# Quarter-array matmuls with transposed outputs in the 512-token steps of a convolution-and-gated-MLP kernel

## The chip, the cores and the metric

The kernel runs on one core of a Trainium2 chip. The metric is the device time of one execution in microseconds; the number given for a kernel is the median of its runs. TensorE is PE in the profile, its weight loads are PEld, VectorE is DVE, ScalarE is ACT, GpSimd is POOL, and SP is the queue that issues most of the transfers.

## The reference, cut to what matters

```python
# x [8, 4096, 192], weight [8 heads, 7 taps], w_in [192, 2048], w_out [2048, 192], beta [2048]
w   = softmax(weight, axis=-1)                 # one set of taps for each head of 24 channels
a   = causal_conv(x, w)                        # out[t] = sum_k w[head, k] * x[t - 6 + k]
h   = a.reshape(32768, 192) @ w_in             # [32768, 2048]
g   = h * sigmoid(beta * h)
out = g @ w_out                                # [32768, 192]
```

## The kernel before, in words

The 32768 tokens are cut into two streams of 16384 (`NS = 2`, index `s`). At every moment the kernel works on the same stretch of both streams. The 192 channels are split as channel = 3 q + k, with k from 0 to 2 (`NK`) and q from 0 to 63. So the activations of one stream fill 64 partitions in three slices, stream 0 in partitions 0 to 63, and stream 1 in 64 to 127. The weights `w_in_s` and `w_out_s` are kept in bf16 in SBUF; `w_out_s` is divided by beta, since the activation is taken as silu(beta h).

There are 37 steps: 0 and 1 of 128 tokens, 2 to 8 of 256, and 9 to 36 of 512 tokens of each stream. The F dimension of 2048 is worked in 16 chunks of 128 (`NF`, index `fc`). In a step of the main loop, for each chunk:

- `mm1(i, fc)` (L321) makes h for the chunk. The contraction of 192 is three matmuls of 64 rows a stream. The two streams use the two row halves of the array, so a pair of matmuls, 64 rows by 128 columns each, runs side by side and writes two PSUM banks (`ph`, two buffers of two banks).
- ScalarE (L324) turns the two banks at once (128x1024) into `g` in bf16.
- `mm2(i - 1, ...)` (L358) works on the step before. Its stationary operand is a block of `g` (128 tokens), its moving operand `w_out_s` (192 columns). Each contraction of 128 rows is cut into two row halves of 64, which again run side by side: while the upper half adds to one token block, the lower half adds to another (`po`, two buffers of two banks). The two halves then change places, in a second phase. `mm2_plan` spreads these pairs over the 16 chunks of the step: eight pairs a chunk where the step before has 512 tokens, four where it has 256.

`store` (L366, L372) copies a finished pair of token blocks from PSUM to `o_sb` with VectorE, and SP sends it out, tokens on partitions, in rows of 768 bytes. The last step has no step after it; `last` (L381, L384, L385) runs its second product alone, with all 128 rows at once.

VectorE makes the convolution for coming steps: `conv_ops` begins a step with a copy of the halo (L280), then for each tap a scale (L289) or a multiply-add (L291) over `acc`, and the last tap writes `xc`. In 512-token steps each tap is three instructions of 128x512, one for each slice k. `cast_x` (L84) casts loaded x to bf16 (`xb`), `transpose_x` (L95) lets SP transpose it into `xt`, and `load_x` (L78) loads x two tiles of 512 ahead.

The order on every engine is the order of the program (`pin`). VectorE's work is a list (`work`), and `vector_work` hands it out by a budget in nanoseconds: each chunk adds 1307 x tokens / 512, each item takes off its estimated cost, and items may belong to at most two steps ahead. At the end of a step everything that the next step needs is flushed out. Copies out of PSUM stand in VectorE's queue where the program finishes a pair of blocks.

Of the kernel before, what the change touches and what calls it, by code (L numbers as in the profile page):

```python
# [10 lines left out]
FP32 = mybir.dt.float32  # L11
# [8 lines left out]
def kernel(  # L20
# [19 lines left out]
    NS = 2  # L40
    TS = B * S // NS
    TILE = 512
    NB = TILE // 128

    def pin(ins):

        return tc.keep_in_program_order(ins)
# [7 lines left out]
    xt_pool = ctx.enter_context(tc.tile_pool(name="xt", bufs=3))  # L55
    acc_pool = ctx.enter_context(tc.tile_pool(name="acc", bufs=2))
    xc_pool = ctx.enter_context(tc.tile_pool(name="xc", bufs=3))
    g_pool = ctx.enter_context(tc.tile_pool(name="g", bufs=2))
    osb_pool = ctx.enter_context(tc.tile_pool(name="osb", bufs=4))
    psum_h = ctx.enter_context(tc.tile_pool(name="psum_h", bufs=2, space=bass.MemoryType.PSUM))  # L60
    psum_o = ctx.enter_context(tc.tile_pool(name="psum_o", bufs=2, space=bass.MemoryType.PSUM))

    steps = [(0, 128), (128, 128), (256, 256)]
    NP = len(steps)
    steps += [(t, 256) for t in range(TILE, 4 * TILE, 256)]
    steps += [(t, TILE) for t in range(4 * TILE, TS, TILE)]
    n_steps = len(steps)

# [30 lines left out]
    w_in_v = moe_w_in.rearrange("(q k) f -> q k f", k=NK)  # L101
    w_out_f = consts.tile([128, NF, D], FP32, name="w_out_f")
    w_out_s = consts.tile([128, NF, D], BF16, name="w_out_s")
    w_out_v = moe_w_out.rearrange("(c p) d -> p c d", p=128)

    def half_of(s):
        return slice(64 * s, 64 * s + 64)
# [47 lines left out]
    for b in (0, 2):  # L155
        for s in range(NS):
# [5 lines left out]
    ident2 = consts.tile([128, NS, Q], FP32, name="ident2")  # L162
    pin(nc.vector.tensor_tensor(out=ident2, in0=ident[:, None, 0:Q].to_broadcast([128, NS, Q]),
                                in1=ident[:, None, Q:].to_broadcast([128, NS, Q]), op=ALU.add))
    def po_tile():
        return psum_o.tile([128, 2, TILE], FP32, name="po")

    idle = psum_h.tile([128, 2, TILE], FP32, name="ph")

# [57 lines left out]
        else:  # L227
            pin(eng.tensor_scalar_mul(dst, src, rsum))  # L228

    def banks(po):  # L230
        return [po[:, 0, :], po[:, 1, :]]

    new_xt(0)
    pa = po_tile()
    t = transpose_0(pa[:, 0, :], 0)
    take_0(t, 0, act=True)
    warm(4, 128)
    for k in range(2, K):
# [5 lines left out]
        for s in range(NS):  # L244
            copy_w_in(s, HF * s + f, HF * s + f + 512)
    pin(nc.scalar.activation(scrap, one, AF.Silu))
    pb = po_tile()
    b0 = [cv0[:, 0, :], pb[:, 0, :]]
    conv_0(b0, 0)
    evac_0(b0, 0, 0, nc.scalar)  # L250
    evac_0(b0, 0, 1, nc.vector)
# [1 line left out]
    pin(nc.tensor.transpose(beta_ps, beta16, ident[0:NF, 0:NF]))  # L253
    beta = consts.tile([128, NF], FP32, name="beta")
    pin(nc.vector.tensor_copy(beta, beta_ps))
    t = transpose_0(pa[:, 0, :], 1)
    take_0(t, 1)
    halo_0(t, 1)
    rbeta = consts.tile([128, NF], FP32, name="rbeta")
# [3 lines left out]

    def scale_w_out(c):
        pin(nc.vector.tensor_scalar_mul(w_out_s[:, c, :], w_out_f[:, c, :], rbeta[:, c:c + 1]))


    def conv_ops(i):
# [45 lines left out]
                                     scale=beta[:, fcs[h]:fcs[h] + 1]))  # L314

    def mm1(i, fc):
        n = steps[i][1]
        ph = psum_h.tile([128, NS, TILE], FP32, name="ph")
        for kk in range(NK):
            for s in range(NS):  # L320
                pin(nc.tensor.matmul(ph[:, s, 0:n], w_in_s[half_of(s), kk, ts(fc, 128)],  # L321
                                     xc_of[i][half_of(s), kk, 0:n],
                                     start=(kk == 0), stop=(kk == NK - 1)))
        pin(nc.scalar.activation(g_of[i][:, fc, :, 0:n], ph[:, :, 0:n], AF.Silu,  # L324
                                 scale=beta[:, fc:fc + 1]))

    def pairs_of(i):
        nb = steps[i][1] // 128
        if nb == 1:
            return [((0, 0), (1, 0))]  # L330
        return [((s, b), (s, b + 1)) for s in range(NS) for b in range(0, nb, 2)]

    def mm2_plan(i):


        prs = pairs_of(i)
        if len(prs) == 1:
            order = [(prs[0], 0, 2 - 2 * i, 6), (prs[0], 1, 10, 16)]
        elif len(prs) == 2:
            order = [(prs[p], ph, 8 * ph + 4 * p, 8 * ph + 4 * p + 4) for ph in range(2) for p in range(2)]  # L340
        else:
            order = [(prs[2 * h + p], ph, 8 * h + 4 * ph + 2 * p, 8 * h + 4 * ph + 2 * p + 2)
                     for h in range(2) for ph in range(2) for p in range(2)]
        plan = [[] for _ in range(NF)]
        for pr, ph, u0, u1 in order:
            for n in range(NF):
                plan[u0 + n * (u1 - u0) // NF].append((pr, ph, n))
        return plan

    def mm2(i, pr, phase, fc):  # L350
        if phase == 0 and fc == 0:
            po_of[pr] = psum_o.tile([128, 2, TILE], FP32, name="po")
        po = po_of[pr]
        for half in range(2):
            q = half ^ phase
            s, b = pr[q]
            r = half_of(half)
            pin(nc.tensor.matmul(po[:, q, 0:D], g_of[i][r, fc, s, ts(b, 128)], w_out_s[r, fc, :],  # L358
                                 start=(phase == 0 and fc == 0), stop=(phase == 1 and fc == NF - 1)))
        if phase == 1 and fc == NF - 1:  # L360
            store(i, pr, po)

    def store(i, pr, po):
        t0 = steps[i][0]
        o_sb = osb_pool.tile([128, 2, D], FP32, name="o_sb")
        pin(nc.vector.tensor_copy(o_sb, po[:, :, 0:D]))  # L366
        (sa, ba), (sb, bb) = pr
        if sa == sb:
            dst = os_[sa, t0 + 128 * ba:t0 + 128 * (bb + 1), :].rearrange("(b p) d -> p b d", p=128)
        else:  # L370
            dst = os_[:, t0 + 128 * ba:t0 + 128 * (ba + 1), :].rearrange("s p d -> p s d")
        pin(nc.sync.dma_start(out=dst, in_=o_sb))  # L372

    def last(i):

        t0, n = steps[i]
        for s in range(NS):
            for b in range(n // 128):
                po = psum_o.tile([128, 2, TILE], FP32, name="po")
                for fc in range(NF):  # L380
                    pin(nc.tensor.matmul(po[:, 0, 0:D], g_of[i][:, fc, s, ts(b, 128)], w_out_s[:, fc, :],  # L381
                                         start=(fc == 0), stop=(fc == NF - 1)))
                o_sb = osb_pool.tile([128, 2, D], FP32, name="o_sb")
                pin(nc.vector.tensor_copy(o_sb[:, 0, :], po[:, 0, 0:D]))  # L384
                pin(nc.sync.dma_start(out=os_[s, t0 + 128 * b:t0 + 128 * (b + 1), :], in_=o_sb[:, 0, :]))  # L385


# [11 lines left out]
    for i in range(NP, n_steps):  # L399
        j = steps[i][0] // TILE + 1  # L400
        if i == NP + 1 or (i > NP + 1 and steps[i][0] % TILE == 0):
            if j * TILE < TS:
                work += fetch(i, j)
        work += conv_ops(i)
    budget = 0.0

    def vector_work(i, ns, flush=False):


# [4 lines left out]
            work.pop(0)[2]()  # L414
        budget = min(budget, 0.0) if work else 0.0

    EVAC = 560
    for i in range(n_steps):
        plan = mm2_plan(i - 1) if i else [[] for _ in range(NF)]
        g_of[i] = g_pool.tile([128, NF, NS, TILE], BF16, name="g")  # L420
        if i == 0:
            cv1, cv2, cv3 = banks(pb), banks(pa), banks(pb)
            for u in range(NF // 2):
                mm1_pair(0, u)
                if u == 0:
                    t = transpose_0(pb[:, 0, :], 2)
                    take_0(t, 2)
                    halo_0(t, 2)
                elif u == 1:
                    t = transpose_0(pa[:, 0, :], 3)  # L430
                    take_0(t, 3)
                    halo_0(t, 3)
                    conv_0(cv1, 1, 0, 1)
                elif u == 2:
                    conv_0(cv1, 1, 1, 4)
                elif u == 3:
                    conv_0(cv1, 1, 4, K)
                    for s in range(NS):
                        evac_0(cv1, 1, s, nc.vector)
                elif u == 4:  # L440
                    conv_0(cv2, 2, 0, 2)
                elif u == 5:
                    conv_0(cv2, 2, 2, 5)
                    for c in range(4):
                        scale_w_out(c)
                elif u == 6:
                    conv_0(cv2, 2, 5, K)
                    for s in range(NS):
                        evac_0(cv2, 2, s, nc.vector)
                elif u == 7:  # L450
                    for c in range(4, 8):
                        scale_w_out(c)
            continue
        if i < NP:
            for u in range(NF // 2):
# [8 lines left out]
                    for s in range(NS):  # L464
                        evac_0(cv3, 3, s, nc.vector)
                elif i == 1 and u == 6:
                    pt = po_tile()
                    new_xt(1)
                    for b in range(2):
                        t = transpose_0(pt[:, b, :], b, xf_of[1])  # L470
                        pin(nc.vector.tensor_copy(  # L471
                            xt_of[1][:, :, LEAD + 128 * b:LEAD + 128 * b + 128], t))
                elif i == 1 and u == 7:
# [13 lines left out]
        for u in range(NF):  # L487
            mm1(i, u)
            for t in plan[u]:
                mm2(i - 1, *t)  # L490
                if t[1] == 1 and t[2] == NF - 1:
                    budget -= EVAC
            vector_work(i, 1307 * steps[i][1] // TILE, flush=u == NF - 1)
    assert not work
    last(n_steps - 1)
# [28 lines left out]
```

## Time and profile before

| | |
|---|---|
| median of 9 runs | 695.87 us (695.45 to 697.47) |
| profiled execution | 696.23 us, of which the profile's span is 694.4 us |
| granted TensorE clock | 1.00 throughout |
| busy: PE, PEld | 687.1 us (99%), 537.7 us (77%) |
| busy: ACT, DVE | 587.5 us (85%), 542.4 us (78%) |
| DMA, mean over the span | 97 GB/s |

The busy time of a group is the union of its instructions, and the mean ns is the length of one from its start to its end. For TensorE these lengths overlap, since matmuls are pipelined and two run side by side; what counts there is the distance from one start to the next. A figure behind the last bar of a group is the engine's idle time just before its instructions, with what ended most of it. The chain that ended last runs back from the final store; an engine's share of it is the time for which it was what everything else depended on.

### The profile page before, as it was taken

To read this page: it belongs to the slowest core of one execution; us is meant where nothing else is said; L and a number is where in the kernel's file an instruction comes from. 1 tells how busy PE (TensorE), PEld (TensorE's weight loads), DVE (VectorE), ACT (ScalarE), POOL (GpSimd) and SP (SyncE) were. 2 spreads that over 40 slices of the span, in tenths; PEclk is the share of its full clock that TensorE was granted. 3 is DMA by queue.
4 is the path that set the end of the run, shared out by engine and by line. 5 is a ranking of instruction groups with operands and counts; after the bars stand their busy time and mean duration, and the time that the engine had idled before them with its cause. 6 is when DMAs were issued, how large, how long until landed. Compare 5 with 4: busy or idle time off the path is not lost.

```text
span 694.4 us, 25426 instructions
## 1 busy us (share of the span) xinstructions
PE 687.1 (99%) x11561; PEld 537.7 (77%) x11561; DVE 542.4 (78%) x905; ACT 587.5 (85%) x600; POOL 14.5 (2%) x26
## 2 busy tenths in 40 slices
PE   8999999999999999999999999999999999999998
PEld 6699986777777777777777777777777777777777
DVE  4799899999988788778788778797788797785002
ACT  6799999888888888888888888888888888888882
POOL 8000000000000000000000000000000000000000
PEclk9999999999999999999999999999999999999999
DMA  9564333444323334323334233334323432211112
GB/s 221 130 144 116 109 110 94 115 129 123 110 66 104 95 103 115 83 76 104 98 105 115 73 90 100 98 104 116 80 77 104 99 105 70 60 36 47 36 37 69
DMA packets 120364, 67.13 MB, mean 97 GB/s; under 512 B 54224, under 2 KB 119456, under 8 KB 120256
## 3 DMA queue, kind: packets, MB, share of 16 engines
q1 hardware_dynamic: 117776, 61.08, 31.7%
q0 software_dynamic: 2336, 4.33, 2.6%
q8 instruction: 90, 1.47, 0.9%
q14 instruction: 18, 0.15, 0.1%
q10 hardware_dynamic: 144, 0.10, 0.1%
HBM read 28.32 MB, written 25.17 MB: 77 GB/s over the span
## 4 chain that ended last, share of the span: by engine, by line
PE 96%; ACT 2%; DMA 1%; POOL 0%; issue 0%; DVE 0%; POOLq 0%; ACTq 0%
PE po L358 47%; PE ph L321 46%; ACT g L312 2%; PE po L381 2%; DMA x<-in_x_dram 1%; PE ph L308 1%; PE po L217 0%; POOL w_in_s L110 0%; PE po L200 0%; DVE xt L471 0%; POOL sel L143 0%; DVE o_sb L384 0%; POOL ident L145 0%; POOLq L143 0%; POOLq L145 0%
## 5 line engine op out<-in xcount | busy, mean ns | idle before, releaser
L324 ACT ACTIVATE g<-ph,beta 128x1024 bf16<-128x1024 f32 (+1 forms) x544 | 560.9, 1039 | 83.8 <-PE ph L321 80.0
L358 PEld LDWEIGHTS <-g 64*128 64x128 bf16 x7936 | 360.3, 94 | 94.9 <-issue 0.2
L358 PE MATMUL po<-w_out_s,g 64*128 64x192 bf16 x7936 | 427.3, 243 | 0.0
L321 PE MATMUL ph<-xc,w_in_s 64*128 64x512 bf16 (+1 forms) x3264 | 418.7, 357 | 0.3 <-ACT g L312 0.3
L291 DVE SCALAR_TENSOR_TENSOR acc<-xt,tapn,acc 128x512 f32<-128x512 bf16 (+1 forms) x450 | 315.3, 763 | 0.9
L321 PEld LDWEIGHTS <-w_in_s 64*128 64x128 bf16 x3264 | 167.1, 94 | 47.6 <-issue 0.5
L366 DVE COPY o_sb<-po 128x384 f32<-128x384 f32 x124 | 69.0, 557 | 127.3 <-PE po L358 125.4
L291 DVE SCALAR_TENSOR_TENSOR xc<-xt,tapn,acc 128x512 bf16<-128x512 bf16 (+1 forms) x90 | 64.1, 763 | 0.2
L84 DVE CAST xb<-xf 128x768 bf16<-128x768 f32 (+1 forms) x62 | 49.1, 832 | 0.0
L289 DVE TENSOR_SCALAR acc<-xt,tapn 128x512 f32<-128x512 bf16 (+1 forms) x90 | 40.5, 500 | 1.1
L312 ACT ACTIVATE g<-ph,beta 128x256 bf16<-128x256 f32 (+1 forms) x48 | 22.3, 562 | 6.3 <-PE ph L308 6.1
L308 PE MATMUL ph<-xcp,w_in_s 64*128 64x256 bf16 (+1 forms) x144 | 14.8, 309 | 1.1 <-ACT g L312 1.1
L381 PE MATMUL po<-w_out_s,g 128*128 128x192 bf16 x128 | 10.7, 246 | 0.0
L381 PEld LDWEIGHTS <-g 128*128 128x128 bf16 x128 | 10.5, 98 | 0.2 <-issue 0.2
L308 PEld LDWEIGHTS <-w_in_s 64*128 64x128 bf16 x144 | 6.6, 95 | 5.2 <-issue 3.1
L384 DVE COPY o_sb<-po 128x192 f32<-128x192 f32 x8 | 2.9, 358 | 7.6 <-PE po L381 7.6
L228 DVE TENSOR_SCALAR xcp<-po,rsum 128x384 bf16<-128x384 f32 x7 | 4.0, 614 | 5.8 <-PE po L217 5.8
L217 PE MATMUL po<-xr,diag 64*128 64x384 f32 x49 | 8.4, 394 | 0.0
L217 PEld LDWEIGHTS po<-xr,diag 64*128 64x128 f32 x49 | 5.5, 206 | 0.2
L280 DVE COPY xt<-xt 128x18 bf16<-128x18 bf16 x28 | 4.6, 165 | 0.0
L200 PE MATMUL po<-ident,x 128*128 128x128 f32 x12 | 3.0, 376 | 0.9 <-DMA x<-in_x_dram 0.9
L110 POOL DMA_DIRECT2D w_in_s<-in_moe_w_in_dram x6 | 3.8, 646 | 0.0
(47 smaller groups left out, 40.4 us busy)
## 6 DMA issues: line engine op xcount, KB each, us to landing
out_dram<-o_sb SPq DMA_DIRECT2D x124, 192.0 KB, 2.7
xf<-in_x_dram SPq DMA_DIRECT2D x60, 384.0 KB, 4.2
xt<-xb SPq DMA_TRANSPOSE x122, 2.4
w_out_f<-in_moe_w_out_dram POOLq DMA_DIRECT2D x4, 384.0 KB, 6.5
xf<-in_x_dram POOLq DMA_DIRECT2D x4, 192.0 KB, 6.8
w_in_s<-w_in_s POOLq DMA_DIRECT2D x4, 192.0 KB, 7.5
out_dram<-o_sb SPq DMA_DIRECT2D x8, 96.0 KB, 1.6
w_in_s<-in_moe_w_in_dram POOLq DMA_DIRECT2D x4, 144.0 KB, 5.4
```

The source lines that it names most:

```text
L84: pin((eng or nc.vector).tensor_copy(xbf_of[j][:, b0:b1, :, s, :].rearrange("p b k q -> p k b q"), xf_of[j][:, b0:b1, s, :].rearrange("p b ...
L217: pin(nc.tensor.matmul(cv[s][:, 0:NK * 128], diag[half_of(s), k, :, :].rearrange("p s q -> p (s q)"), xr[b][half_of(s), :, k:k + 128], sta ...
L280: pin(nc.vector.tensor_copy(xt[:, :, LEAD - PAD:LEAD], xt_of[j - 1][:, :, TILE + LEAD - PAD:]))
L289: pin(nc.vector.tensor_scalar_mul(a, src, w))
L291: pin(nc.vector.scalar_tensor_tensor(out=xc_of[i][:, k0:k1, 0:n] if k == K - 1 else a, in0=src, scalar=w, in1=a, op0=ALU.mult, op1=ALU.add))
L308: pin(nc.tensor.matmul(ph[:, h, 0:NS * n], w_in_s[half_of(h), kk, ts(fcs[h], 128)], xc_of[i][half_of(h), :, kk, :], start=(kk == 0), stop= ...
L312: pin(nc.scalar.activation(g_of[i][:, fcs[h], :, 0:n], ph[:, h, 0:NS * n].rearrange("p (s t) -> p s t", s=NS), AF.Silu, scale=beta[:, fcs[ ...
L321: pin(nc.tensor.matmul(ph[:, s, 0:n], w_in_s[half_of(s), kk, ts(fc, 128)], xc_of[i][half_of(s), kk, 0:n], start=(kk == 0), stop=(kk == NK ...
L324: pin(nc.scalar.activation(g_of[i][:, fc, :, 0:n], ph[:, :, 0:n], AF.Silu, scale=beta[:, fc:fc + 1]))
L358: pin(nc.tensor.matmul(po[:, q, 0:D], g_of[i][r, fc, s, ts(b, 128)], w_out_s[r, fc, :], start=(phase == 0 and fc == 0), stop=(phase == 1 a ...
L366: pin(nc.vector.tensor_copy(o_sb, po[:, :, 0:D]))
L381: pin(nc.tensor.matmul(po[:, 0, 0:D], g_of[i][:, fc, s, ts(b, 128)], w_out_s[:, fc, :], start=(fc == 0), stop=(fc == NF - 1)))
```

## The change

In the 512-token steps both products are issued on quarters of the array, 64 rows by 64 columns.

- **First product.** From step 10 on, `mm1` splits each matmul of 128 output columns into two of 64, so that a chunk has twelve matmuls of 64x64 by 512 in place of six of 64x128 by 512, in the order: first column half for both streams, second column half for both streams.
- **Second product, for steps 9 to 35 (run in steps 10 to 36).** The operands change places: the stationary operand is a 64x64 piece of `w_out_q`, and the moving operand is `g`, 512 tokens of one stream. `w_out_q` is a second copy of `w_out_s`, with the 192 output columns parted into three thirds by d mod 3 (`part_w_out`, twelve VectorE copies of 128x256, queued for step 10). The result in PSUM is transposed: output channels on partitions, stream 0 in partitions 0 to 63, stream 1 in 64 to 127, tokens along the bank. One bank holds one third.
- **Turns.** A turn has up to four matmuls: for each stream (column half) and each row half. The two row halves work on different thirds: the upper one in the order A, B, C, the lower one in the order C, A, B and 8 turns later (`LAG = 8`), so that they never add to one bank at once. Every chunk issues 3 turns (`NM`), 48 a step. What is left over at the end is issued in `last` before the last step's product.
- **Output.** When a third is done, VectorE transposes its bank in blocks of 32x32 (128x512 f32) into `o_sb`, with a stride of three elements. After the last third SP sends the step out in four transfers, one for each group of 32 partitions, in pieces of 384 bytes.
- **Elsewhere.** PSUM for outputs is four single-bank buffers in place of two double ones; in the steps up to 9 the copy of a pair of blocks is two copies of 128x192 instead of one of 128x384. `g` is two fixed tiles used in turn. The budget takes (tokens + 60) / 0.96 ns for a transposing copy.

```diff
+    w_out_q = consts.tile([128, NF, NM, D // NM], BF16, name="w_out_q")
...
+    def part_w_out(c, m):
+        pin(nc.vector.tensor_copy(w_out_q[:, c:c + 4, m, :],
+                                  w_out_s[:, c:c + 4, :].rearrange("p c (q m) -> p c q m", m=NM)[:, :, :, m]))
...
+        parts = [(0, 128)] if i <= NQ else [(0, 64), (64, 128)]
         for kk in range(NK):
-            for s in range(NS):
-                pin(nc.tensor.matmul(ph[:, s, 0:n], w_in_s[half_of(s), kk, ts(fc, 128)],
-                                     xc_of[i][half_of(s), kk, 0:n],
-                                     start=(kk == 0), stop=(kk == NK - 1)))
+            for m0, m1 in parts:
+                for s in range(NS):
+                    pin(nc.tensor.matmul(ph[m0:m1, s, 0:n],
+                                         w_in_s[half_of(s), kk, 128 * fc + m0:128 * fc + m1],
+                                         xc_of[i][half_of(s), kk, 0:n],
+                                         start=(kk == 0), stop=(kk == NK - 1)))
...
+    A, B_, C = range(NM)
+    LAG = 8
+    turns = [[], [None] * LAG]
+    for i in range(NQ, n_steps - 1):
+        for r, thirds in enumerate(((A, B_, C), (C, A, B_))):
+            turns[r] += [(i, m, fc) for m in thirds for fc in range(NF)]
+    turns[0] += [None] * LAG
+    turns = list(zip(*turns))
+
+    def mm2_quarters(count):
+        for _ in range(count):
+            turn = turns.pop(0)
+            for s in range(NS):
+                for r in range(2):
+                    if turn[r] is None:
+                        continue
+                    i, m, fc = turn[r]
+                    if (i, m) not in po_of:
+                        po_of[i, m] = po_bank()
+                    first = r == (m == C)
+                    n = steps[i][1]
+                    pin(nc.tensor.matmul(po_of[i, m][half_of(s), 0:n], w_out_q[half_of(r), fc, m, :],
+                                         g_of[i][half_of(r), fc, s, 0:n],
+                                         start=(first and fc == 0), stop=(not first and fc == NF - 1)))
+            for r in range(2):
+                if turn[r] is not None:
+                    i, m, fc = turn[r]
+                    if fc == NF - 1 and r != (m == C):
+                        take_third(i, m)
...
+    def take_third(i, m):
+        nonlocal budget
+        n = steps[i][1]
+        if i not in osb_of:
+            osb_of[i] = osb_pool.tile([128, TILE // L, L, NM], FP32, name="o_sb", bufs=2)
+        pin(nc.vector.transpose(osb_of[i][:, 0:n // L, :, m],
+                                po_of[i, m][:, 0:n].rearrange("p (b l) -> p b l", l=L)))
+        budget -= (n + 60) / 0.96
+        if m != B_:
+            return
         t0, n = steps[i]
         for s in range(NS):
+            dst = os_[s, t0:t0 + n, :].rearrange("(b l) (g d) -> g l b d", l=L, g=2)
+            for g in range(2):
+                p = 64 * s + L * g
+                pin(nc.sync.dma_start(out=dst[g],
+                                      in_=osb_of[i][p:p + L, 0:n // L, :, :].rearrange("p b l m -> p b (l m)")))
...
     def last(i):
         t0, n = steps[i]
+        mm2_quarters(len(turns))
...
+        if i == NQ + 1:
+            work += [(i, 330, lambda c=c, m=m: part_w_out(c, m)) for c in range(0, NF, 4) for m in range(NM)]
         work += conv_ops(i)
...
-                    budget -= EVAC
+                    budget -= 2 * (D + 60) / 0.96
+            if i > NQ:
+                mm2_quarters(NM)
             vector_work(i, 1307 * steps[i][1] // TILE, flush=u == NF - 1)
```

## The prediction

> **What bounds the kernel now.** I read the page's busy shares, then the chain that ended last, then the timeline inside one 512-token step, then the Vector queue where these steps begin. The page:
>
> ```profile
> span 694.4 us, 25426 instructions
> PE 687.1 (99%) x11561; PEld 537.7 (77%) x11561; DVE 542.4 (78%) x905; ACT 587.5 (85%) x600; POOL 14.5 (2%) x26
> PEclk9999999999999999999999999999999999999999
> PE 96%; ACT 2%; DMA 1%; POOL 0%; issue 0%; DVE 0%; POOLq 0%; ACTq 0%
> PE po L358 47%; PE ph L321 46%; ACT g L312 2%; PE po L381 2%; DMA x<-in_x_dram 1%; PE ph L308 1%; PE po L217 0%; POOL w_in_s L110 0%; PE po L200 0%; DVE xt L471 0%; POOL sel L143 0%; DVE o_sb L384 0%; POOL ident L145 0%; POOLq L143 0%; POOLq L145 0%
> L324 ACT ACTIVATE g<-ph,beta 128x1024 bf16<-128x1024 f32 (+1 forms) x544 | 560.9, 1039 | 83.8 <-PE ph L321 80.0
> L358 PE MATMUL po<-w_out_s,g 64*128 64x192 bf16 x7936 | 427.3, 243 | 0.0
> L321 PE MATMUL ph<-xc,w_in_s 64*128 64x512 bf16 (+1 forms) x3264 | 418.7, 357 | 0.3 <-ACT g L312 0.3
> ```
>
> TensorE is busy 99% at full clock, and 93% of the chain are its two matmul lines, with 0.3 us of waits on other engines ahead of them. ACT waits 80 us for TensorE and is not the limit. Nothing but TensorE's own time per step can make the kernel faster, and that time is nearly all streaming, as the timeline from 300 us shows (start, length):
>
> ```profile
> 300.13 0.83 PE L321 MATMUL ph<-xc,w_in_s 64*128 64x512 bf16 x6
> 300.78 0.84 PE L358 MATMUL po<-w_out_s,g 64*128 64x192 bf16 x16
> 301.44 0.83 PE L321 MATMUL ph<-xc,w_in_s 64*128 64x512 bf16 x6
> 302.08 0.84 PE L358 MATMUL po<-w_out_s,g 64*128 64x192 bf16 x16
> ```
>
> One F-chunk takes 300.13 to 301.44, 1.307 us: three pairs of 512 columns (0.65 us), then eight pairs of 192 (0.66 us). The trace's start times give it more finely: 215.8 ns from a 512-column pair to the next (mean of 1223), 82.5 ns for 192 columns (mean of 4283). The two lie on a line of 0.4166 ns a column plus 2.5 ns. So each "turn" (a set of matmuls that run side by side) costs its columns plus 2.5 ns, and a chunk pays 11 of these. The last step, with one matmul of all 128 rows a turn, has 82.6 ns for 192 columns: the 2.5 ns is the same for one tile and for two.
>
> **The change, part by part** (the 27 steps 10 to 36, 16 chunks each, run in quarters).
>
> *Turns.* w_out's matmuls take 192 of 64x64 by 512 columns a step in place of 256 of 64x128 by 192. Four at a time these are 48 turns of 512 columns, 3 a chunk; before, 8 of 192. The columns are equal (1536), the turns fall from 8 to 3. The first product keeps 3 turns: twelve quarter matmuls, four at a time. A chunk is 6 x 215.8 = 1294.9 ns in place of 3 x 215.8 + 8 x 82.5 = 1307.4. That is -12.5 ns x 16 x 27 = -5.4 us, if four quarters run as two halves do. No row shows quarters, so this is the unknown that decides. There are 27 x 16 x 6 = 2592 such turns, and each ns a turn is 2.6 us.
>
> *Weight loads.* Their number a turn goes from two to four, of 64 columns instead of 128. Row: a 64x128 load lasts 94 ns, two overlap in every 82.5 ns, and a half's load starts 2 ns after that half's own matmul, beside it:
>
> ```profile
> 676.03 0.84 PE L358 MATMUL po<-w_out_s,g 64*128 64x192 bf16 x16
> 676.03 0.61 PEld L358 LDWEIGHTS <-g 64*128 64x128 bf16 x14
> ```
>
> Fourteen loads of 94 ns are 1.3 us of work in 0.61 us. At that row four loads fit in 215.8 ns even if only the two row halves overlap and a half's two loads go one after the other (188 ns): cost 0. The Trainium skill speaks against it twice. "TensorEngine Tiling (Array Packing)", Tiling Modes, says that column tiling switches fast weight load off; "TensorE: Matmul & The Clock Gate", LDWEIGHTS, gives an unaided load as columns over 1.2 GHz, so I estimate 53.3 ns for 64 columns. Four in strict series are 213.3 ns, which only just fits; with the 2.5 ns each they are 223.3 ns, and the sum gains 7.5 x 2592 = +19.4 us. The second page also says (Part 3) that a load overlaps running matmuls only in another row group; by that every turn would grow by 53 ns, +138 us. The rows above contradict this for halves. Ends: 0 and +138; I take 0, since the nearest row (64 rows, two tiles, twice the columns) shows loads overlapping each other and their own half's matmul.
>
> *The lag.* The lower row half runs 8 turns behind, so the first 8 turns and the last 8 fill only half the array. A chunk always issues 3 turns, so the whole surplus comes out before the last step's product: 8 x 215.8 = +1.7 us, exposed.
>
> *Vector engine, steady.* Three transposes of 128x512 replace four copies of 128x384 (557 ns). Row: a copy from PSUM took 358 ns for 192 and 557 ns for 384 elements, 1.04 ns an element, so 690 ns for 512: 2.1 us a step against 2.2. If a transpose ran at half that rate, it would be 1.2 us, 3.7 a step. DVE is busy 34.05 us in the two steps from 240 to 282.84 us, 16.6 a step; without copies 14.4 of a step of 20.7, so a transpose may cost up to 2.1 us before DVE binds. Cost 0, covered by that slack; twice the row is covered too.
>
> *Vector engine at the start of the quarters.* Twelve strided copies that part w_out (128x256) are queued just ahead of the convolution for step 10, and copies of the short steps are split in two (0.36 us each alone; I take +0.1 us a pair). Here the cover is thin (the first four lines are the Vector queue, the last is TensorE at the start of step 10):
>
> ```profile
> 99.62 0.56 DVE L366 COPY o_sb<-po 128x384 f32<-128x384 f32 x1 [0.32 <-PE po L358]
> 100.09 0.48 DVE L289 TENSOR_SCALAR acc<-xt,tapn 128x512 f32<-128x512 bf16 x1
> 100.49 10.02 DVE L291 SCALAR_TENSOR_TENSOR acc<-xt,tapn,acc 128x512 f32<-128x512 bf16 x15
> 110.42 2.07 DVE L291 SCALAR_TENSOR_TENSOR xc<-xt,tapn,acc 128x512 bf16<-128x512 bf16 x3
> 115.68 0.82 PE L321 MATMUL ph<-xc,w_in_s 64*128 64x512 bf16 x6
> ```
>
> xc is done at 112.5, and step 10 starts at 115.68: 3.2 us of slack. A 128x768 cast takes 0.77 us back to back, so 256 elements take 0.26 to 0.33; I take 0.28. In the built order four of the twelve fall before the copy at 99.62, in what was idle time or is passed to later; eight come after. From 100.2: 8 x 0.28, halo 0.2, three scales 1.2, fifteen taps 10.1, then one pair of copies 0.6 that now stands before the last taps: 114.5. xc's three parts then come at about 115.3, 116.0, 116.7, against a need at 115.7, 115.9, 116.1: a stall of about 0.5 us. Bounds: 0 (copies in the old idle time) and 1.5 (0.36 us each). Later steps have 8 us and more of slack, less 4.
>
> *Queues.* SP issues four output transfers a step as before, but together after the last third, 32 partitions by 16 pieces of 384 bytes in place of rows of 768. Two o_sb buffers leave each a step to land. DMA share in steady steps is 0.36; if the outputs' packets cost twice, it stays under 0.5. Input loads and xt transposes are queued behind them and run a tile ahead: 0. ACT's own work is unchanged; a chunk of 1.295 us still covers 1.114. Mode switch: the existing one before L381 left a gap of 0.16 us; one more at step 10: +0.1.
>
> *Sum.* -5.4 + 1.7 + 0.5 + 0.1 = -3.1 us. The profiled execution took 696.23 us (span 694.4, 1.8 around it): 693.1, span 691.3. It lies 0.36 above the median of 695.87, so the forecast is 692.8.
>
> **Rivals.**
>
> 1. *Quarters keep step less well than halves* (slower). Place: every turn on TensorE, through loads that go one after another. It decides from (5.4 - 2.3) / 2592 = 1.2 ns a turn: a turn over 217.0 ns is a loss. With loads in series as estimated above: 712. For it: no row shows four tiles, and the margin is 0.6% of a turn. Against: loads overlap freely now, and the 2.5 ns did not grow from one tile to two.
> 2. *Loads not hidden at all*: 53 ns a turn, about 831. Against: the load rows above.
> 3. *Vector engine becomes the bound*: at four times the row's rate per element a transpose costs some 2.3 us, 14.4 + 6.9 = 21.3 against 20.7, +0.6 x 27 = 16 us, about 709. For: nothing in this trace is such a transpose, and steps 9 to 11 leave DVE no idle time. Against: 6 us of room a step later.
> 4. *No difference*: the turns gain, but a stall of 1.5 us at step 10, late thirds in the next two steps, or 1 ns a turn eat it: 694.5 to 697.
>
> **How the numbers follow.** A difference under 0.2% (1.4 us) can't be told from none. The forecast's own case, 691.5 to 694.4: 0.55. Rival 4: 0.09. Rival 1: 0.22. Rival 3 and other waits: 0.09. Rival 2: 0.05. Faster 0.55, same 0.09, slower 0.36. The likeliest case's own range is 691.5 to 694.4. For 8 in 10 the range goes from 690.5 (a turn 0.7 ns shorter and no stall) to 713, which takes in rival 4, most of rival 1 and half of rival 3.
>
> **What would show it.** Right: TensorE turns of four at 215.8 ns, chunks of 1.295 us, L336 on ACT at that pace, a surplus of 1.7 us before the last step's product, under 1 us of TensorE waiting for xc at about 116 us, transposes of 0.65 to 0.75 us. Wrong: chunks over 1.302 us with no wait named (rival 1), TensorE waiting for DVE in every step (rival 3), load time as long as matmul time (rival 2).

## The result and the profile after

The changed kernel takes 691.90 us (median of 10 runs, 691.59 to 693.85) against 695.87 of the kernel before (31 runs, 695.15 to 698.66). The ratio is 0.9943, with a 95% interval of 0.9933 to 0.9953. That is 4.0 us less; the forecast was 692.8, 3.1 us less. The profiled execution took 691.75 us with a span of 690.0, against 696.23 and 694.4.

The page of the changed kernel (first product now L332, second L412, the short steps' second product L366, the last step's L450, activation L336):

```profile
span 690.0 us, 27516 instructions
PE 683.8 (99%) x12425; PEld 429.6 (62%) x12425; DVE 553.5 (80%) x906; ACT 589.0 (85%) x600; POOL 14.5 (2%) x26
PEclk9999999999999999999999999999999999999999
PE 96%; ACT 2%; DMA 1%; POOL 0%; issue 0%; DVE 0%; POOLq 0%; ACTq 0%
L336 ACT ACTIVATE g<-ph,beta 128x1024 bf16<-128x1024 f32 (+1 forms) x544 | 562.5, 1039 | 78.1 <-PE ph L332 68.4
L332 PE MATMUL ph<-xc,w_in_s 64*64 64x512 bf16 (+2 forms) x5856 | 613.2, 366 | 0.3 <-ACT g L319 0.3
L412 PE MATMUL po<-g,w_out_q 64*64 64x512 bf16 x5184 | 552.2, 376 | 0.0
L332 PEld LDWEIGHTS <-w_in_s 64*64 64x64 bf16 (+1 forms) x5856 | 257.4, 104 | 152.9 <-issue 0.6
L412 PEld LDWEIGHTS <-w_out_q 64*64 64x64 bf16 x5184 | 242.0, 105 | 89.0
L429 DVE STREAM_TRANSPOSE o_sb<-po 128x512 f32<-128x512 f32 x81 | 72.0, 888 | 110.4 <-PE po L412 110.4
```

TensorE still has 99% and 96% of the chain, at full clock, and its two lines wait 0.3 us in all. So the kernel is bound as it was, and a step has become shorter. The busy time of L332 and L412 adds up to far more than the span, since matmuls of the two products now overlap in time (below). A step's length is best read from the distance of the first activations of neighbouring steps: 20.72 us in every step from 10 on, 20.92 before. The 16 chunks of such a step take 1295.0 ns each, as forecast, and 12.4 ns less than before: five turns fewer, at 2.5 ns each.

The path through the kernel, cut at those first activations, shows where the 4.5 us of the two spans lie:

| stretch | before | after | difference |
|---|---|---|---|
| start to step 3 | 36.57 us | 34.99 us | -1.58 |
| steps 3 to 9 | 80.03 us | 81.37 us | +1.34 |
| steps 10 to 35 | 544.01 us | 538.72 us | -5.29 |
| step 36 to the end | 33.83 us | 34.88 us | +1.05 |

The third line is the forecast's main term (26 of the 27 steps; the 27th is in the last line). The first two lines were in no case of the forecast, and nearly cancel.

The timeline of the changed kernel at 300 us (start, length) does not look like the one before, with one product after the other:

```profile
299.94 0.41 PE L412 MATMUL po<-g,w_out_q 64*64 64x512 bf16 x4
300.16 0.38 PE L332 MATMUL ph<-xc,w_in_s 64*64 64x512 bf16 x2
300.19 0.38 PE L412 MATMUL po<-g,w_out_q 64*64 64x512 bf16 x2
300.37 0.38 PE L332 MATMUL ph<-xc,w_in_s 64*64 64x512 bf16 x2
300.40 0.38 PE L412 MATMUL po<-g,w_out_q 64*64 64x512 bf16 x2
300.59 0.42 PE L332 MATMUL ph<-xc,w_in_s 64*64 64x512 bf16 x4
```

Two matmuls start together (6 to 7 ns apart), and the other two of the set some 30 ns later; the next set follows 0.22 us after. In four of six sets the two pairs belong to different products. In the program, though, the twelve matmuls of a product stand in one block. Pairs of the later block thus start while pairs of the earlier one still have turns to come: one half of the array is ahead of the other by two turns. Six such sets make a chunk, in the 1295 ns measured.

Which half is ahead can be read from the semaphores in the trace. The first matmul of a chunk in the program waits for ScalarE and belongs to the upper row half; the last one releases ScalarE and belongs to the lower. In the first chunk of step 10 the last starts 0.47 us after the first, as in lockstep; from the third chunk on it starts 0.03 us before it. So the lower half, which has no second product to do in the first eight turns, moved two turns ahead there and stayed so. The lines at the start of step 10 show it move: in the third of them, two matmuls of the second chunk's first product start before two of the first chunk's second product, which stand ahead of them in the program.

```profile
115.65 0.60 PE L332 MATMUL ph<-xc,w_in_s 64*64 64x512 bf16 x8
116.08 0.60 PE L412 MATMUL po<-g,w_out_q 64*64 64x512 bf16 x4
116.42 0.41 PE L332 MATMUL ph<-xc,w_in_s 64*64 64x512 bf16 x2
116.52 0.38 PE L412 MATMUL po<-g,w_out_q 64*64 64x512 bf16 x2
```

### The profile page after: what moved, and what is told of

Same layout as the page of the kernel before. It is cut to its first block, busy times and chain, and to the rows that moved or that the text cites. A ratio compares the mean times of both kernels' runs of the same rounds, so it can differ in the third digit from the quotient of the medians.

```text
span 690.0 us, 27516 instructions
## 1 busy us (share of the span) xinstructions
PE 683.8 (99%) x12425; PEld 429.6 (62%) x12425; DVE 553.5 (80%) x906; ACT 589.0 (85%) x600; POOL 14.5 (2%) x26
## 4 chain that ended last, share of the span: by engine, by line
PE 96%; ACT 2%; DMA 1%; POOL 0%; issue 0%; DVE 0%; POOLq 0%; ACTq 0%
PE ph L332 47%; PE po L412 41%; PE po L366 6%; ACT g L319 2%; PE po L450 2%; DMA x<-in_x_dram 1%; PE ph L315 1%; PE po L223 0%; POOL w_in_s L113 0%; PE po L206 0%; POOL sel L146 0%; DVE o_sp L372 0%; POOL ident L148 0%; POOLq L146 0%; POOLq L148 0%
## 5 line engine op out<-in xcount | busy, mean ns | idle before, releaser
L336 ACT ACTIVATE g<-ph,beta 128x1024 bf16<-128x1024 f32 (+1 forms) x544 | 562.5, 1039 | 78.1 <-PE ph L332 68.4
L332 PE MATMUL ph<-xc,w_in_s 64*64 64x512 bf16 (+2 forms) x5856 | 613.2, 366 | 0.3 <-ACT g L319 0.3
L412 PE MATMUL po<-g,w_out_q 64*64 64x512 bf16 x5184 | 552.2, 376 | 0.0
L332 PEld LDWEIGHTS <-w_in_s 64*64 64x64 bf16 (+1 forms) x5856 | 257.4, 104 | 152.9 <-issue 0.6
L298 DVE SCALAR_TENSOR_TENSOR acc<-xt,tapn,acc 128x512 f32<-128x512 bf16 (+1 forms) x450 | 311.3, 759 | 0.9
L412 PEld LDWEIGHTS <-w_out_q 64*64 64x64 bf16 x5184 | 242.0, 105 | 89.0
L429 DVE STREAM_TRANSPOSE o_sb<-po 128x512 f32<-128x512 f32 x81 | 72.0, 888 | 110.4 <-PE po L412 110.4
L366 PE MATMUL po<-w_out_s,g 64*128 64x192 bf16 x1024 | 65.1, 243 | 0.0
L366 PEld LDWEIGHTS <-g 64*128 64x128 bf16 x1024 | 49.3, 94 | 5.5
L372 DVE COPY o_sp<-po 128x192 f32<-128x192 f32 x40 | 12.6, 352 | 10.3 <-PE po L450 4.4
L450 PEld LDWEIGHTS <-g 128*128 128x128 bf16 x128 | 10.5, 98 | 0.4 <-issue 0.4
L450 PE MATMUL po<-w_out_s,g 128*128 128x192 bf16 x128 | 10.7, 246 | 0.0
L315 PEld LDWEIGHTS <-w_in_s 64*128 64x128 bf16 x144 | 6.4, 94 | 5.1 <-issue 3.4
```

Of the source, the lines that this page charges most:

```text
L298: pin(nc.vector.scalar_tensor_tensor(out=xc_of[i][:, k0:k1, 0:n] if k == K - 1 else a, in0=src, scalar=w, in1=a, op0=ALU.mult, op1=ALU.add))
L315: pin(nc.tensor.matmul(ph[:, h, 0:NS * n], w_in_s[half_of(h), kk, ts(fcs[h], 128)], xc_of[i][half_of(h), :, kk, :], start=(kk == 0), stop= ...
L332: pin(nc.tensor.matmul(ph[m0:m1, s, 0:n], w_in_s[half_of(s), kk, 128 * fc + m0:128 * fc + m1], xc_of[i][half_of(s), kk, 0:n], start=(kk == ...
L366: pin(nc.tensor.matmul(po[q][:, 0:D], g_of[i][r, fc, s, ts(b, 128)], w_out_s[r, fc, :], start=(phase == 0 and fc == 0), stop=(phase == 1 a ...
L412: pin(nc.tensor.matmul(po_of[i, m][half_of(s), 0:n], w_out_q[half_of(r), fc, m, :], g_of[i][half_of(r), fc, s, 0:n], start=(first and fc = ...
L429: pin(nc.vector.transpose(osb_of[i][:, 0:n // L, :, m], po_of[i, m][:, 0:n].rearrange("p (b l) -> p b l", l=L)))
```

## The experiments

Each is timed against the kernel before on the same chip, and ratios are to that.

### e4: the first product left in halves

```diff
-        parts = [(0, 128)] if i <= NQ else [(0, 64), (64, 128)]
+        parts = [(0, 128)]
```

> The changed kernel, with the first product left in row halves of 64x128 throughout, so that each chunk goes from halves to quarters and back. Theory: the first product gains nothing by itself from quarters (3 turns either way), and is in quarters only because a change of tiling mode drains the array; 2 changes a chunk, 864 in all, at 0.1 to 0.16 us (the gap of 0.16 us where the last step's product begins) are 86 to 138 us: 778 to 830. Rival: a change of mode costs nothing, and the quartered first product is neutral: 691.9.

Measured: 791.97 us, ratio 1.1382 (1.1367 to 1.1396). Its timeline, weight loads and matmuls (in brackets the idle time before, and what ended it):

```profile
300.05 0.33 PEld L332 LDWEIGHTS <-w_in_s 64*128 64x128 bf16 x6 [0.41 <-issue]
300.05 0.82 PE L332 MATMUL ph<-xc,w_in_s 64*128 64x512 bf16 x6
300.80 0.36 PEld L412 LDWEIGHTS <-w_out_q 64*64 64x64 bf16 x12 [0.42 <-issue]
300.80 0.84 PE L412 MATMUL po<-g,w_out_q 64*64 64x512 bf16 x12
301.57 0.33 PEld L332 LDWEIGHTS <-w_in_s 64*128 64x128 bf16 x6 [0.41 <-issue]
301.58 0.82 PE L332 MATMUL ph<-xc,w_in_s 64*128 64x512 bf16 x6
```

A chunk takes 300.05 to 301.58 us, 1.526 us by the step of 24.41 us. Loads for the other tiling don't start until the matmuls of the one before are nearly through: 0.41 us without a load, at each change. (24.41 - 20.72) / 32 = 115 ns a change. So the first product is in quarters for one reason: it must be in the same tiling as its neighbour. Alone it saves no turn, and left out it costs 100 us. That agrees with the Trainium skill, "TensorEngine Tiling (Array Packing)", Tiling Modes, by which a change of mode drains the array; this run gives the price.

### e5: the second product in pieces of 256 columns

```diff
-            for s in range(NS):
+            for c0, c1, s in [(c, c + 256, s) for c in (0, 256) for s in range(NS)]:
...
-                    pin(nc.tensor.matmul(po_of[i, m][half_of(s), 0:n], w_out_q[half_of(r), fc, m, :],
-                                         g_of[i][half_of(r), fc, s, 0:n],
+                    pin(nc.tensor.matmul(po_of[i, m][half_of(s), c0:c1], w_out_q[half_of(r), fc, m, :],
+                                         g_of[i][half_of(r), fc, s, c0:c1],
...
```

> The changed kernel, with every quarter matmul of the second product cut into two of 256 columns: columns as they were, 48 turns and 192 weight loads more a step. Theory: a turn costs its columns plus 2.5 ns, and loads overlap one another; then 48 x 2.5 x 27 = +3.2 us, 695.1. This leaves a load of 105 ns (its row after) just under a turn of 109 ns; should one row half's two loads go one after the other (210 ns a turn), a turn grows by 101 ns and the kernel by 96 x 101 x 27 = 262 us, 954; with all four in series at 53.3 ns each (estimate of the skill's page) 213 ns and about the same. Rival on the gain: it came from fewer or shorter weight loads and not from fewer turns; then the loss here goes by the loads, far over 3 us.

Measured: 696.52 us, ratio 1.0015 (1.0003 to 1.0028); the span is 694.6, 4.6 over that of the changed kernel. Groups of its trace:

```profile
L412 PE MATMUL po<-g,w_out_q 64*64 64x256 bf16 x10368 | 440.2, 269 | 0.0
L412 PEld LDWEIGHTS <-w_out_q 64*64 64x64 bf16 x10368 | 378.4, 107 | 33.7 <-issue 0.3
```

Steps take 20.84 us, 0.12 more than the changed kernel's. 48 more turns at 2.5 ns are 0.12 us: the price of a turn holds to the last digit shown, and 27 x 0.12 = 3.2 us is the theory's sum. It also rules out a limit by loads: 192 more of them, 107 ns long, with four to a turn of 109 ns, cost nothing beside the turns. So the fall from 11 turns to 6 is what made a chunk shorter, and the columns' price is the same in halves, quarters and at half the length.

The rest of the 4.6 us is in three steps that take about 21.1 us (0.9 us together) and in the last stretch (0.5 us beyond its own 0.12). In each of the three steps TensorE stops once: at 217.08, 319.25 and 486.26 us the next weight load comes 0.25 to 0.41 us after the one before has ended, with no wait in the profile ("issue"). What held it stays open. After the first of these stops the lower half has lost its lead of two turns (0.43 us), which fits the longer last stretch.

### e1: single PSUM banks alone

The kernel before with `po_bank` and `po_banks` of the changed one, and nothing else of it.

```diff
-psum_o = ctx.enter_context(tc.tile_pool(name="psum_o", bufs=2, ...))
+psum_o = ctx.enter_context(tc.tile_pool(name="psum_o", bufs=4, ...))
...
-        return psum_o.tile([128, 2, TILE], FP32, name="po")
+        return psum_o.tile([128, TILE], FP32, name="po")
```

> The kernel before with one part of the change alone: outputs in four single PSUM banks in place of two double ones, and with that two copies of 128x192 for one of 128x384. The trace after begins step 3 at 34.07 us against 35.66, which the forecast had not counted. Theory: the double tile made the two start-up transposes of step 1 and their copies wait for one another, so single banks give about 1.1 to 1.6 us, and this kernel takes 694.3 to 694.8. Rival: the start only varies with the arrival of x, or the gain came from the fixed g tiles; then 695.9, within 0.3.

Measured: 694.93 us, ratio 0.9987 (0.9977 to 0.9997). Its first activation of step 3 comes at 35.41 us, 1.15 us earlier than before. Steps 3 to 9 take 80.02 us (80.03 before), and the later ones 20.92 as before, except step 10 (0.19 longer). Most of the 1.15 us is in step 1, which takes 9.18 us in place of 10.19. It takes 9.1 to 9.2 us in all nine traces with single banks, and 10.2 in both with double tiles (before and e8). So about 1.0 us of the gain has nothing to do with quarters. The waits of the kernel before up to 37 us name the place (who waits, on whom, us, times, longest):

```profile
PEld po L200 <- DVE xt L471: 0.8, 1, 0.8
PE po L200 <- DVE xt L471: 0.6, 1, 0.6
```

There the second start-up transpose waited for the copy of the first out of the other bank of one double tile. In the changed kernel's waits these two lines are missing.

The rival of a start that varies is true of the rest. Step 0 takes 7.1 to 10.0 us in the eleven traces. It takes 7.4 to 10.0 even in the six of the changed kernel, e4 to e7 and e9, which do the same work up to step 9; in these TensorE waits for the DMA of x for 0.7 us (changed kernel) to 1.8 us (e7) there. The changed kernel's step 0 is 0.60 us shorter than before, and that is not shown to come from the change.

### e8: fixed g tiles alone

```diff
-        g_of[i] = g_pool.tile([128, NF, NS, TILE], BF16, name="g")
+        g_of[i] = gs[i % 2]
```

> The kernel before with one part of the change alone: g in two fixed tiles used in turn in place of a pool of two. Theory: a second wait on each activation, of no effect where TensorE sets the pace and of some 16 ns an activation in steps 3 to 9 (112 activations): +1.3 to +1.8 us, 697.2 to 697.7. Rival: nothing, 695.9.

Measured: 697.03 us, ratio 1.0017 (1.0008 to 1.0026). Steps 5 to 7 take 10.72 us as in the changed kernel (10.545 before), step 9 takes 16.69 (16.27). Steps 3 to 9 together take 81.34 us in place of 80.03, +1.31, as the theory has it. In the 512-token steps from 10 on nothing changes (20.92). The whole is +1.0 by the medians, 0.6 by the spans: in this trace the start is 0.6 us earlier (step 3's first activation at 35.94), with a short step 0 (7.11 us), which e1 shows to vary by more than that.

### e2: g rotating up to step 10, in the changed kernel

```diff
-        g_of[i] = gs[i % 2]
+        g_of[i] = g_pool.tile([128, NF, NS, TILE], BF16, name="g") if i <= NQ + 1 else g_of[i - 2]
```

> The changed kernel, with g rotating from a pool up to step 10 and the last two tiles then kept and used in turn. Theory: with fixed g tiles every activation waits for an earlier one of ScalarE as well as for TensorE, which costs a waiting instruction each (530 in the trace after, 34 before) and some 16 ns in steps 3 to 9, where ScalarE sets the pace (10.72 us a step against 10.55, 16.70 against 16.28). Taking it away up to step 10 gives 1.3 to 1.5 us: 690.5. Rival: those steps are slower for another reason, the split copies or the single banks; then 691.9 as the changed kernel.

Measured: 691.11 us, ratio 0.9934 (0.9918 to 0.9949), span 689.4. Steps 5 to 7 are back at 10.545 us and step 9 at 16.37 (0.1 over the kernel before). ScalarE's timeline in steps 5 to 7, 22 activations each, of the kernel before, of e8, of the changed kernel and of e2, in this order:

```profile
65.68 14.52 ACT L324 ACTIVATE g<-ph,beta 128x512 bf16<-128x512 f32 x22
```

```profile
65.42 14.77 ACT L324 ACTIVATE g<-ph,beta 128x512 bf16<-128x512 f32 x22
```

```profile
65.82 14.77 ACT L336 ACTIVATE g<-ph,beta 128x512 bf16<-128x512 f32 x22
```

```profile
65.78 14.54 ACT L336 ACTIVATE g<-ph,beta 128x512 bf16<-128x512 f32 x22
```

The two with fixed tiles need 14.77 us, the two with rotating ones 14.52 to 14.54. And what stands between, from the list of line 336 of the changed kernel (operation, count, shortest, median and longest in ns, first and last start):

```profile
L336 ACTq EVENT_SEMAPHORE  x530: 17/17/17, 34.6 to 674.4; - x177
```

With rotating tiles an activation waits for TensorE's semaphore alone. With fixed ones it waits for ScalarE's own as well, and the wait for TensorE then is an instruction by itself, of 17 ns. In steps 3 to 9 there are 98 of these, and 7 in the kernel before. The cost isn't 17 ns each: by whole steps it is 11 ns an activation in steps 5 to 7 (10.72 against 10.545 us) and 28 ns in step 9. Steps 3 to 9 grow by 1.31 us in e8 and shrink by 1.25 in e2; the table's +1.34 is this, up to 0.1.

The theory was not right that ScalarE sets the pace in all of these steps. In a 256-token step of the kernel before, a chunk is three turns of 256 columns and four of 192, 3 x 109.2 + 4 x 82.5 = 657.6 ns, and activations come 657 to 658 ns apart: that is TensorE's own pace. In step 9 the same sum is 977 ns and a chunk takes 1013, so there TensorE is not the limit. With fixed tiles the activations of steps 5 to 7 come 657 and 683 ns apart in turn. The two engines were nearly even there, and the second wait made ScalarE the slower one.

### e9 and e10: the changed kernel and e2 once more, on one chip

> The changed kernel again, on one chip with the next: 691.9, by the first measurement.

> The changed kernel with g rotating up to step 10, again: by the sum of its steps 3 to 9 (80.1 us against 81.4 in the trace of the changed kernel) 1.2 us less than the changed kernel of the same call. If steps 3 to 9 were only lucky: no difference.

Measured: e9 693.43 us (ratio 0.9956, 0.9940 to 0.9972), e10 691.89 (0.9938, 0.9922 to 0.9955). The spans of the profiled executions are 689.9 and 689.4. Steps 3 to 9 are 1.24 us shorter again. But in both pairs of traces some is given back: at the start 0.36 us (e2) and 0.44 (e10, step 3's first activation at 35.39 against 34.95), which is within what the start varies by itself, and 0.27 in the last stretch. There the trace of e2 has lost about 0.28 us of the lower half's lead, since the end of step 14. So e2 is the fastest kernel here by 0.5 to 0.6 us in the traces; its intervals overlap those of the changed kernel, and the runs alone don't tell the two apart.

### e6 and e7: the transposing copy two and three times

```diff
+        for _ in range(2):      # e7: 3
             pin(nc.vector.transpose(osb_of[i][:, 0:n // L, :, m], ...))
```

> The changed kernel, with each transposing copy out of PSUM issued twice. A step has three more of 888 ns. Theory: VectorE's work is covered, up to some 2.1 us a third; 1.8 us fit, and only the first steps of the quarters, where VectorE is late, may lose: 691.9 to 693.5. Rival: VectorE is already near the limit through the order of its queue; then some 2.7 us a step, 27 x 2.7 = +70 us, 760.

> The changed kernel, with each transposing copy issued three times: 2.7 us a third, 8.0 us a step. Theory: VectorE becomes the bound, with 14.4 us of other work and 8.0 in a step of 20.72: 22.4, +1.7 us x 25 to 27 steps less the lead that it has: 720 to 737. Rival: copies that follow one another overlap by about 0.08 us and the queue keeps its lead: 692 to 700.

Measured: e6 696.93 us (ratio 1.0003, 0.9987 to 1.0020), e7 743.67 (1.0676, 1.0657 to 1.0696). TensorE's waits for VectorE, of e6 and then of e7:

```profile
PE po L412 <- DVE o_sb L430: 2.3, 3, 2.0
```

```profile
PE po L412 <- DVE o_sb L430: 41.5, 25, 3.8
```

e6 has steps of 20.72 us except for steps 13 to 15, which take 21.29, 23.03 and 21.09: 3.2 us in all. So in the steady steps two transposes a third are covered, and the loss is where VectorE has not yet caught up: `xc` is ready 7 to 16 us ahead of its step in these three, and 23 us later on. (The budget still counts one copy a third.) The size was misjudged: 3.2 us there and 0.5 in the last stretch, where the lower half's lead is gone, in place of 0 to 1.6. Another 0.8 us of the 4.5 in the spans is in the start, which the edit doesn't touch. e7 has steps of about 22.5 us, near the 22.4 of the sum. VectorE is the bound there, in 25 waits of 1.7 us; it lost 52 us, somewhat more than the 28 to 45 expected, since the first quarter steps took up to 26.35 us. Again 2.1 us of it are in the start.

## Why the prediction was right, point by point

- **Turns.** Forecast 1294.9 ns a chunk and -5.4 us; measured 1295.0 ns, and 27 x 0.20 = 5.4 us. The step that decided, that four quarters keep step as two halves do, was an inference from one and two tiles. The trace confirms it for four, and e5 confirms the 2.5 ns at another length. Rival 1 fails: the sets of step after step are 215 or 216 ns apart, 215.8 in the mean.
- **Weight loads.** Taken at 0, and 0 it is, though the size was off: a load of 64 columns takes 105 ns and one of 128 took 94. Of the two rules that the prediction weighed here, the first (on its page it stands under Tile-to-Partition Mapping, Restrictions, and not under Tiling Modes) fits in its direction, since half the columns are not loaded faster; that it is the cause no run here shows. The second fails: e5's loads overlap matmuls of their own row half, four of 107 ns in 109 ns. The estimate of 53 ns each in series, 213 ns for four, is ruled out: four fitted in half that. Rival 2 fails with it.
- **The lag.** Forecast +1.7 us for eight turns; it cost six, 1.3 us. From the start of step 10 to L450, the time over 27 steps of 20.72 is 1.39 us: six turns of 215.8 ns and 0.09 for the change of tiling before L450. The lower half, two turns ahead since the start of step 10, is through two turns sooner:

```profile
674.20 2.11 PE L412 MATMUL po<-g,w_out_q 64*64 64x512 bf16 x24
676.24 10.73 PE L450 MATMUL po<-w_out_s,g 128*128 128x192 bf16 x128
```

  The forecast had the halves move in lockstep, so this term was too large by 0.43 us. Over 27 steps of 20.92 the kernel before had 0.20 us in the same stretch: 0.11 for its change of tiling, and a step 10 that was 0.09 longer than the others.
- **The stall at step 10.** Forecast 0.5 us, measured none that the waits name. The twelve copies came every 0.20 us, not 0.28, and the last eight began at 99.47 us, 0.7 earlier than the forecast's 100.2. The changed kernel's VectorE queue:

```profile
97.55 0.89 DVE L271 COPY w_out_q<-w_out_s 128x256 bf16<-128x256 bf16 x4
98.93 0.62 DVE L372 COPY o_sp<-po 128x192 f32<-128x192 f32 x2 [0.50 <-PE po L366]
99.47 1.70 DVE L271 COPY w_out_q<-w_out_s 128x256 bf16<-128x256 bf16 x8
112.94 2.07 DVE L298 SCALAR_TENSOR_TENSOR xc<-xt,tapn,acc 128x512 bf16<-128x512 bf16 x3
```

  xc is ready at 115.01 us, and step 10 begins at 115.41. The slack of 3.2 us is down to 0.4, so the pinch was real. Part of what is left was lent by ScalarE's slower steps: in e2, where they are as before, the slack is 0.04 us.
- **VectorE, steady.** A transpose takes 888 ns, not 690. The cover was 2.1 us a third, so the error cost nothing; e6 and e7 put the limit between two transposes a third (covered) and three (not). Rival 3 fails for the change, and e6 shows how near it was in steps 13 to 15.
- **Queues.** An output transfer of 384-byte pieces lands in 5.0 us at the median, against 2.7. Nothing waits for it in the steady steps. The DMA share there is 0.38 in place of 0.36.

What the forecast missed are side effects of two edits in the steps before 10. Single banks gave 1.0 us at the start (e1), and fixed g tiles took 1.3 us in steps 3 to 9 (e8, e2). The fixed tiles were not costed at all: "ACT's own work is unchanged" was true of the activations and not of the waits. And "Nothing but TensorE's own time per step can make the kernel faster" was too much, since a shorter start did. A step 0 shorter by 0.6 us, which varies by itself, came on top. The table's first two lines come to -0.24 us: that they cancel is luck. The forecast's 0.1 us for a change of tiling at step 10 lies in the second of them and can't be told apart there (e8, without that change, has 1.31 us of the 1.34).

So the forecast's sum of -3.1 us against -4.5 in the spans is 0.5 (no stall), 0.4 (lag), 0.2 (the two lines), 0.1 (the change of tiling, counted in them), 0.1 (step 10 of the kernel before), and a remainder within rounding.

## What to carry to other kernels

Where a matmul stream is already dense, count turns: a set of side-by-side matmuls costs its columns plus 2.5 ns here, whatever its tiling, so longer moving operands are worth a little and only that. Neighbouring products must then share a tiling, since each change cost 115 ns, nine times what a chunk had gained. Cost also the edits that only serve the main one (tile ownership, PSUM layout) in the stages where another engine is as near the bound: there one more wait on each activation took back 1.3 us, a quarter of the 5.4 gained.

## What was not expected of the hardware

- The two row halves are not in lockstep: matmuls of one half start before earlier ones of the other in the program's order, by two turns (0.43 us) in this kernel. It was one half's lack of work in the first eight turns that let it get ahead, and it could use two of the eight; what sets that number is not shown. Nothing in the trace of before showed it, as both halves always had equal work.
- A weight load of 64x64 lasts 105 ns, longer than one of 64x128 (94 ns), and still costs no time at four in 109 ns.
- A 32x32-block transpose of 128x512 f32 from PSUM into a stride of three takes 888 ns, where 690 was estimated for a plain copy of that size from copies of 192 and 384 elements. Strided bf16 copies of 128x256, 0.28 us long each, follow one another every 0.20 us.
